# One input load for the small vectors, a later start for the f16 scores, and spare matrix products in foreseen gaps

## The chip, the core and the metric

The kernel runs on one core of one Trainium2 chip. The core has a matrix engine (TensorE, PE in the profile), three elementwise engines (VectorE or DVE, ScalarE or ACT, GpSimd or POOL), a queue engine that mostly issues transfers (SyncE or SP), and 16 DMA engines. Each engine works through its own instructions in order and waits on the others through semaphores. The metric is the device time of one execution in microseconds (us), as the median of several runs. Lower is better.

## The reference

Attention over 8 batches, 12 heads, 448 tokens and head size 64, with a root-mean-square norm on q and k, feeds a gated feed-forward step with a token shift. All in f32:

```
q_n = q / sqrt(mean(q*q) + 1e-6) * g_q          # same for k with g_k
attn = softmax(q_n @ k_n^T / sqrt(64))
x    = (attn @ v), heads side by side            # 8 x 448 x 768
x_prev = x shifted by one token
xk = mu_k*x + (1-mu_k)*x_prev ;  xr = mu_r*x + (1-mu_r)*x_prev
kk = relu(xk @ w_k)**2                           # 768 -> 1024
out = sigmoid(xr @ w_r) * (kk @ w_v)             # 768 -> 768, 1024 -> 768
```

The weights arrive as 8-byte floats. g_q and g_k are vectors of 64, mu_k and mu_r of 768.

## The kernel before

**Tiles.** The 96 heads are taken as 48 pairs `i` (two heads of a batch) and 24 quads `u` (two pairs). A batch has three quads. The scores of a quad come in seven groups `gi` of 128 query rows for two heads, so `groups` has 168 entries; `gi < 21` belongs to the quads `u < U32 = 3`. Those first three quads are computed in f32 (one product per term); all later ones split each operand into two f16 parts and use three products per term.

**Stages.** `setup` loads g_q and g_k, forms their product and a scale from it with some twenty small DVE instructions on the tile `gm`, and writes a per-partition column `gc`. `mu_stats` loads mu_k and mu_r through the ACT queue as many 4-byte pieces and derives bounds in `muu`, `mucol` and `smu`. `load` fetches k and q of each quad, `stats` forms the sums of squares (`sst`) and their inverse roots (`ss`), `preps` scales k and q into `nat` and transposes them (`turn`, on TensorE for `u < PE_T`, by DMA afterwards) into `stk`. `scores` multiplies, `expo` takes the maximum and the exponential, `probs` and `probs_pe` normalise and transpose the result into `pT`; all groups of the first three quads take `probs_pe`. `attends` multiplies by v (tiles `vf`, `vh`, `vl`) into `x`. `mix` forms the shifted mixes through `df` into `xk` and `xr`. `wload`, `weights`, `wscale` and `wsplit` convert 20 weight tiles (`raw`, `kk`, `wk`, `wr`, `wv`, `wf`) to f16 pairs; for the bounds, `weights` also multiplies each tile with itself into the bank `pg`. `moe` runs the three large products, batch by batch: `xk` with `wk` first, then, once all weights are split and `xr` is there, `xr` with `wr` and `kk` with `wv`, and stores `o`.

**Accumulators.** All products land in one ring of eight banks named `ps`, shared out by use: at most five for scores and TensorE transposes (`sc`), two for `moe`, two for attention output, one for `pg`, and so on. `scores` takes two `sc` banks for each group; before, it took them for the first quads when more than `SC_KEEP = 2` were free. A transpose of `turn` or `probs_pe` needs one `sc` bank.

**Order.** Each stage is a generator that yields its next operation. `Plan` keeps a modelled clock for every engine and the modelled end of every access to a tile. `run` picks the operation with the smallest key: the later of its engine's clock and its data, plus a margin, less `PS = 0.1` ns for each point of priority. `emit` writes the instruction and moves the clocks. So the whole order on all engines is fixed when the kernel is built, and each engine then runs its list as the data arrive. All instructions but a few carry line 289 of `emit` in the profile. The priority of `attends` contains `BOOST_A`, that of the weights `W_GAP` (a smaller `W_GAP` raises it sooner).

Of the kernel before, what the change touches and what calls it, by code (L numbers as in the profile page):

```python
# [7 lines left out]
F32 = mybir.dt.float32  # L8
# [8 lines left out]
P = 128  # L17
HD = 64
# [45 lines left out]
PRIO_M = 400  # L64
BOOST_K = 500
BOOST_R = 500
BOOST_A = 0
BOOST_W = 300
BOOST_Q = 600
SLACK_S = 3  # L70
# [8 lines left out]
Q_DVE = 1  # L79
V_POOL = True  # L80
PE_T = 6
U32 = 3
V_SIDE = 2
SWITCH = 600
# [7 lines left out]
LEAD_V = 1  # L92
LEAD_W = 1
PE_P = range(1, 21, 2)
SC_KEEP = 2
TR_COST = 130
W_GAP = 7e3
W_PUSH = 0.03
NEWTON_ON = "DVE"
OP_SLOW = 1.0  # L100
# [118 lines left out]
        return lambda form=None, **kw: Op(self.name, f, {k: aps(x) if hasattr(x, "shape") else x for k, x in kw.items()}, form)  # L219


class Plan:
    LAT = 35

    def __init__(self, tc):
        self.tc = tc
        self.clk = dict.fromkeys(("PE", "DVE", "ACT", "POOL", "SP"), 0.0)
        self.last, self.use, self.threads = {}, {}, []
        self.form, self.dma_free, self.acc, self.n = None, {"SP": 0.0, "ACT": 0.0}, False, 0
        self.held = {"DVE": [], "POOL": []}  # L230

    def margin(self, form):
        if form == "moe":
# [49 lines left out]
    def emit(self, ops):  # L283
        e = ops[0].eng
        rel = self.ready(ops)
        s = max(self.clk[e], rel)
        for op in ops:
            with self.tc.issue_after(self.last[e].ins) if e in self.last else nullcontext():
                r = op.fn(op.kw["out"], op.kw["value"]) if op.fn.__name__ == "memset" else op.fn(**op.kw)  # L289
            self.last[e] = r  # L290
        if e == "PE":
            form, cost = ops[0].form
            form = MODE.get(form, 0)
            cost *= PE_SLOW
            if form != self.form:
                s += 105
            self.form = form
            self.clk[e] = s + cost
            fin = s + cost + 190
            for op in ops:  # L300
                self.note(op, fin)
        elif ops[0].fn.__name__.startswith("dma"):
            op = ops[0]
            x = op.kw["out"]
            n = width(x) * x.ap[0][1]
            if "transpose" in op.fn.__name__:
                w, iss, tot = n / 128 * 1.21, 1700, 4000
            else:
                w, iss, tot = n / 55, 350, 3300
            w, tot = w * DMA_SLOW, tot * DMA_SLOW  # L310
            other = "ACT" if e == "SP" else "SP"
            if e == "ACT":
                end = s + (375 if n > 60000 else 610)
            else:
                end = max(s + iss, min(self.dma_free[e] - 1200, s + 4000))
            self.clk[e] = end + 35
            begin = max(self.dma_free[e], s + tot - w - 900)
            both = DMA_SHARE * min(w, max(0.0, self.dma_free[other] - begin))
            self.dma_free[e] = begin + w + both
            self.dma_free[other] += both  # L320
            self.note(op, self.dma_free[e] + 900)
        else:
            op = ops[0]
            pace, dur = (x * OP_SLOW for x in price(op))
            if e == "ACT":
                acc = op.kw.get("accum_out") is not None
                if acc and self.acc:
                    s = max(s, self.clk[e] + ACC_GAP)
                self.acc = acc
            if e in self.held and shares(op):  # L330
                for a, b in self.held["DVE" if e == "POOL" else "POOL"]:
                    if a <= s < b - 190:
                        s = b - 190
                h = self.held[e]
                h.append((s, s + dur))
                del h[:-16]
            self.clk[e] = s + pace
            self.note(op, s + dur)
        self.n += 1

    def run(self):
        while self.threads:
# [29 lines left out]
class Ring:  # L372
# [21 lines left out]
    def get(self, early=False):  # L394
        ok = lambda: [x for x in self.free if early or isinstance(x, str)]
        while not ok():
            yield ok
        tag = ok()[0]
        self.free = [x for x in self.free if x is not tag]
        if not isinstance(tag, str):  # L400
            self.of[id(tag)] = (tag, None, tag)
            return tag
        pool = self.more.get(tag) or (self.pool() if callable(self.pool) else self.pool)
        t = pool.tile(self.shape, self.dtype, name=tag, bufs=1)
        name = aps(t).tensor.name
        self.of[id(t)] = (tag, name, t)
        old = self.plan.use.get("slot " + tag)
        if old:
            self.plan.use[name, 0], self.plan.use[name, 1] = [(0, 1 << 30, old, True, False)], [(0, 1 << 30, old, True, False)]
        return t  # L410
# [43 lines left out]
            yield V.scalar_tensor_tensor(out=y, in0=t, scalar=1.5, in1=y, op0=ALU.add, op1=ALU.mult)  # L454


def attn_moe_kernel(tc, q, k, v, g_q, g_k, mu_k, mu_r, w_k, w_v, w_r, out):
    nc = tc.nc
    B, H = 2 * out.shape[0], D_MODEL // HD
    NP = H // 2  # L460
# [12 lines left out]
    banks = {n: Share(psum, *c) for n, c in (("sc", SC_SHARE), ("mm", MM_SHARE), ("ot", OT_SHARE), ("wz", WZ_SHARE), ("pg", PG_SHARE), ("df", DF_SHARE))}  # L473

    ident16 = const.tile([P, P], BF16, name="ident16")
    gq = const.tile([P, HD], F32, name="gq")
    gk = const.tile([P, HD], F32, name="gk")
    mu = const.tile([P, 2, 2, ND], F32, name="mu")
    gm = const.tile([P, 8], F32, name="gm")
    G = gq  # L480
    gc = const.tile([P, 1], F32, name="gc")
# [14 lines left out]
    NQ, NPAIR, NSS, NSL, NVB = len(quads), len(pairs), 4 * NT, (NT + 1) // 2, 2 * NT  # L496
    VFREE = [const.tile([P, NVB, HD], F32, name="vf%d" % n) for n in range(VF_BUFS)]

    st = {"wdone": 0, "g": 0, "moe": 0, "vl": 0, "gm": False, "mus": False, "want": "xk", "sg": 0, "su": 0, "pu": 0, "vi": 0, "wkeys": 0, "kdone": 0, "zq": 0, "tq": 0, "lu": 0}
    LD, SS, VF, VV, TQ, PT, BS, BSC, XT, XK, XKN, XR, CNT, OS, CARRY, FR = {}, {}, {}, {}, {}, {}, {}, {}, {}, {}, {}, {}, {}, {}, {}, {}  # L500

    plan.st = st
# [62 lines left out]
    ring_sum = [small.tile([P, 12], F32, name="sums%d" % n, bufs=1) for n in range(6)]  # L565

    def setup():
        yield SP.dma_start(out=gq, in_=g_q.partition_broadcast(P))
        yield SP.dma_start(out=gk, in_=g_k.partition_broadcast(P))
        yield A.copy(out=ident16, in_=ident)  # L570
        yield V.memset(out=ones, value=1.0)
        st["vf"] = True
        yield V.scalar_tensor_tensor(out=G, in0=gq, scalar=1.0 / float(HD) ** 0.5, in1=gk, op0=ALU.mult, op1=ALU.mult)
# [11 lines left out]
        st["gm"] = True  # L585

    def mu_stats():
        yield from until(lambda: st["lu"] >= 1 and len(RAW))
        yield A.dma_start(out=mu[:, 0, 0, :], in_=mu_k.rearrange("(t p) -> p t", p=P))
        yield A.dma_start(out=mu[:, 1, 0, :], in_=mu_r.rearrange("(t p) -> p t", p=P))  # L590
        yield V.tensor_scalar(out=mu[:, :, 1, :], in0=mu[:, :, 0, :], scalar1=-1.0, scalar2=1.0, op0=ALU.mult, op1=ALU.add)
        u = small.tile([P, 2, ND], F32, name="muu")
        u2 = small.tile([P, 2, ND], F32, name="muu2")
# [205 lines left out]

    def scores():  # L800
        for gi, (u, x, t0) in enumerate(groups):
            yield from until(lambda: u in TQ and len(banks["sc"].free) > (SC_KEEP if u < U32 or gi in PE_P else 1) and not st["zq"])
            tp = None
            if u < U32 or gi in PE_P:
# [77 lines left out]
    def probs_pe(u, x, t0, sums, tp):  # L882
# [8 lines left out]
        for a0 in range(0, NT, 4):  # L891
            m = min(4, NT - a0)
            st["zq"] += 1
            z = yield from banks["sc"].get()
            st["zq"] -= 1
            yield [T.transpose(form=("tr", TR_COST * m), out=z[:, a * P:(a + 1) * P], in_=tf[:, (a0 + a) * P:(a0 + a + 1) * P], identity=ident) for a in range(m)]
            src = z[:, 0:m * P].rearrange("p (a c) -> p a c", c=P)
            if u < U32:
                dst = whole(PTQ[:, :, :])[:, a0:a0 + m, c0:c0 + P]
                yield A.copy(out=dst, in_=src) if plan.pick("ACT", "DVE") == "ACT" else V.tensor_copy(out=dst, in_=src)  # L900
            else:
                hi, lo = (PTQ[:, h + a0:h + a0 + m, c0:c0 + P] for h in (0, NT))
                yield A.copy(out=hi, in_=src)
                yield V.tensor_tensor(out=lo, in0=src, in1=hi, op=ALU.subtract)
            banks["sc"].put(z)
        R["nat"].put(tp)
        for i in (2 * u, 2 * u + 1) if t0 == NT - 1 else (2 * u + x,):
            CNT[i] += 1
# [100 lines left out]
    def weights():  # L1009
        for nm, w, kt, c, ci in WT:  # L1010
            if c == 0:
                pg = yield from banks["pg"].get()
            last = ci + 1 in (NF, NF + ND, NW)
            nb = 2 if ci < NF else 1
            if last:
# [6 lines left out]
            for h in range(2):  # L1022
# [8 lines left out]
                yield V.scalar_tensor_tensor(out=fi[:, cols], in0=z.bitcast(I32), scalar=3, in1=fi[:, cols], op0=ALU.logical_shift_left, op1=ALU.bitwise_or)  # L1031
                banks["wz"].put(zb)
                R["raw"].put(raw)
            w16 = f.bitcast(BF16).rearrange("p (i n two) -> p i n two", two=2, n=P)[:, :, :, 1]
            yield [T.matmul(form=("w", 110 * kt), out=pg[:, c % nb * P:(c % nb + 1) * P], lhsT=w16[:, i, :], rhs=w16[:, i, :], start=(c == 0 and i == 0), stop=(last and i == kt - 1)) for i in range(kt)]
            if last:
                plan.spawn(wscale(nm, kt, ci - c, ci + 1, pg, nb * P), wprio)

# [158 lines left out]
    ctx.close()  # L1197


_INS = ["q", "k", "v", "g_q", "g_k", "moe_mu_k", "moe_mu_r", "moe_w_k", "moe_w_v", "moe_w_r"]  # L1200


def layouts(inputs):
# [31 lines left out]
    for name in ("moe_w_k", "moe_w_v", "moe_w_r"):  # L1235
        w = np.asarray(inputs[name])
        a = w.reshape(2, -1, P, w.shape[1] // P, P).transpose(3, 0, 2, 1, 4)
        laid[name] = np.ascontiguousarray(a).reshape(*a.shape[:3], -1)
    return {**laid, "q": qd, "k": kd, "v": vd.reshape(b * h // 2, P, 2 * NT * HD)}


def tokens_back(o, b):
# [29 lines left out]
```

## Time and profile before

| | |
|---|---|
| median of 3 runs | 1003.53 us (1002.27 to 1003.83) |
| the profiled execution: time | 1002.68 us |
| the profiled execution: span of the instructions | 1000.9 us |
| mean granted TensorE clock | 0.973 of full speed |
| instructions | 18138 |
| busy: TensorE, ScalarE, GpSimd, VectorE | 91%, 78%, 68%, 66% |
| packets moved, mean rate | 359357, 156 GB/s |

The span runs from the first to the last instruction; the time holds 1.8 us more. Busy time counts an engine as busy while an instruction of its own is under way; for TensorE, the ends of the products are modelled and they overlap. In the rows below, `SPq` and `ACTq` are the queues on which transfers are issued, `PEld` is the loading of TensorE's stationary operand, and `[3.74 <-DVE nat L289]` means that the engine was idle for 3.74 us before the row and that a DVE instruction writing `nat` ended that wait. `x7` at the end counts the instructions merged into the row.

### The profile page before, as it was taken

What the parts mean: (1) busy time and instruction counts of PE and PEld (TensorE: products, weight loads), DVE (VectorE), ACT (ScalarE), POOL (GpSimd) and SP (SyncE); (2) the same over time, 40 slices, a digit from 0 to 9 for tenths busy, and PEclk for the clock granted to TensorE, in tenths of its full rate; (3) what the DMA queues carried; (4) which work ended last, traced back from release to release, by engine and by line L of the source; (5) the groups of instructions that cost most, each with busy time, mean ns of one, the idle gap of its engine ahead of it and who ended that gap; (6) DMA issues with size and microseconds to landing.
All of it is one profiled execution on the core that took longest, in us unless ns stands there. A gap on an engine that the chain in (4) does not pass through costs nothing. (4 is left out here: it accounts for less than half of the span.)

```text
span 1000.9 us, 18138 instructions
## 1 busy us (share of the span) xinstructions
PE 911.1 (91%) x6048; PEld 478.5 (48%) x6048; DVE 663.7 (66%) x1816; ACT 781.2 (78%) x1740; POOL 675.9 (68%) x744
## 2 busy tenths in 40 slices
PE   0687859799899999999999999989998999999998
PEld 0443434355444555445444555445544555565564
DVE  4797887778875887688875878777866875012000
ACT  2587889889997999999997999999889977424200
POOL 2578898957797777978797777968588624635400
PEclk9798969989999999999999999999999999999999
DMA  5444566499978999799988999999977992100000
GB/s 191 150 153 126 174 183 131 79 200 187 231 145 170 223 215 225 155 205 210 232 168 157 219 208 224 187 185 196 217 170 150 182 182 69 37 16 32 1 33 31
DMA packets 359357, 156.38 MB, mean 156 GB/s; under 512 B 338272, under 2 KB 338272, under 8 KB 359264
## 3 DMA queue, kind: packets, MB, share of 16 engines
q1 hardware_dynamic: 357552, 154.76, 70.5%
q8 instruction: 47, 0.77, 0.3%
q10 hardware_dynamic: 1712, 0.47, 0.2%
q14 instruction: 46, 0.38, 0.1%
HBM read 60.23 MB, written 11.01 MB: 71 GB/s over the span
## 5 line engine op out<-in xcount | busy, mean ns | idle before, releaser
L289 PE MATMUL ps<-wv,kk 128*128 128x384 f16 x1344 | 233.8, 326 | 1.4 <-DVE df L289 1.4
L289 PE MATMUL ps<-xk,wk 128*128 128x448 f16 x1152 | 226.1, 353 | 2.8 <-DVE nat L289 2.2
L289 DVE TENSOR_REDUCE sums<-ps 128x1 f32<-128x448 f32 x336 | 192.3, 613 | 20.4 <-PE ps L289 20.2
L289 ACT ACTIVATE ps<-ps,sums 128x448 f32<-128x448 f32 x294 | 189.3, 646 | 18.3 <-DVE sums L289 16.7
L289 DVE SCALAR_TENSOR_TENSOR nat<-ps,sums,nat 128x448 f16<-128x448 f32 x242 | 158.7, 677 | 56.3 <-ACT nat L289 55.8
L289 ACT ACTIVATE nat<-ps,sums 128x448 f16<-128x448 f32 (+1 forms) x274 | 173.1, 679 | 22.6 <-DVE sums L289 15.0
L289 PE MATMUL ps<-wr,xr 128*128 128x384 f16 x1008 | 180.3, 330 | 2.4 <-DVE o L289 1.3
L289 PEld LDWEIGHTS <-kk 128*128 128x128 f16 (+1 forms) x1350 | 128.0, 98 | 97.6 <-issue 17.1
L289 PEld LDWEIGHTS <-wk 128*128 128x128 f16 (+1 forms) x1194 | 113.4, 99 | 113.5 <-issue 14.2
L289 PE MATMUL ps<-stk 64*128 64x448 f16 (+3 forms) x1104 | 131.5, 384 | 22.0 <-DVE nat L289 9.4
L289 PEld LDWEIGHTS <-xr 128*128 128x128 f16 x1008 | 96.8, 99 | 76.5 <-issue 16.6
L289 DVE SCALAR_TENSOR_TENSOR o<-o,ps 128x384 f32<-128x384 f32 x56 | 30.7, 548 | 108.5 <-PE ps L289 108.3
L289 DVE SCALAR_TENSOR_TENSOR df<-x,bsc,ps 128x448 f32<-128x448 f32 x96 | 63.8, 674 | 54.1 <-ACT ps L289 46.6
L289 PE MATMUL ps<-pT,vh 128*64 128x448 f16 x588 | 93.2, 361 | 0.2
L289 ACT ACTIVATE o<-ps,bsc 128x384 f32<-128x384 f32 x48 | 28.9, 603 | 76.5 <-PE ps L289 76.5
L289 POOL TENSOR_TENSOR qk<-qk,ss 128x896 f32<-128x896 f32 x36 | 60.9, 1693 | 19.1 <-DVE ss L289 15.9
L289 PEld LDWEIGHTS <-stk 64*128 64x128 f16 x1008 | 35.7, 97 | 76.4 <-issue 50.0
L289 POOL TENSOR_SCALAR o<-o,bsc 128x768 f32<-128x768 f32 x24 | 21.8, 910 | 71.7 <-DVE o L289 54.3
L289 POOL TENSOR_TENSOR nat<-nat 128x448 f32<-128x448 f32 x38 | 43.1, 1135 | 38.7 <-ACT nat L289 19.9
L289 ACT ACTIVATE ps<-x,bsc 128x448 f32<-128x448 f32 x96 | 64.4, 683 | 0.8 <-DVE nat L289 0.7
L289 POOL TENSOR_TENSOR xr<-df,xr 128x448 f16<-128x448 f32 x48 | 49.5, 1042 | 21.8 <-ACT xr L289 21.7
L289 POOL TENSOR_SCALAR vf<-vf,bstat 128x896 f32<-128x896 f32 x42 | 42.8, 1019 | 28.2 <-DVE bstat L289 16.3
(172 smaller groups left out, 1553.2 us busy)
## 6 DMA issues: line engine op xcount, KB each, us to landing
vf<-in_v_dram SPq DMA_DIRECT2D x42, 448.0 KB, 4.2
out_dram<-o SPq DMA_DIRECT2D x28, 384.0 KB, 2.8
qk<-in_k_dram SPq DMA_DIRECT2D x23, 448.0 KB, 4.4
qk<-in_q_dram SPq DMA_DIRECT2D x22, 448.0 KB, 4.3
raw<-in_moe_w_v_dram SPq DMA_DIRECT2D x12, 512.0 KB, 3.9
raw<-in_moe_w_r_dram SPq DMA_DIRECT2D x12, 384.0 KB, 3.2
kk<-in_moe_w_k_dram SPq DMA_DIRECT2D x8, 384.0 KB, 3.3
raw<-in_moe_w_k_dram SPq DMA_DIRECT2D x8, 384.0 KB, 3.2
```

Source lines behind the costliest of these rows:

```text
L289: r = op.fn(op.kw["out"], op.kw["value"]) if op.fn.__name__ == "memset" else op.fn(**op.kw)
```

## The change

It has three parts.

1. **One load.** g_q, g_k, mu_k and mu_r are laid side by side on the host, for each of the 128 partitions, in one array `small` of 152 f32 columns. One transfer on SP's queue brings it into the tile `few`; `gq`, `gk` and `mu` are views of it. The two broadcast loads on SP's queue and the two loads on ACT's queue are gone. `mu_stats` starts once `setup` has ended (`st["gm"]`), where it had waited for the progress of other loads.
2. **Order.** `BOOST_A` goes from 0 to 700, `SC_KEEP` from 2 to 1, `W_GAP` from 7000 to 6000. The scores of group 21 and later wait until all 21 groups of the first three quads have ended `probs_pe` (`st["pz"]`).
3. **Spare products.** When `emit` writes a TensorE operation that the plan's clocks place later than the end of the one before, `warm` puts 128x128 bf16 products of the identity with itself ahead of it: one for every 57 ns of 0.8 times the foreseen gap less 200 ns. While a weight matrix is being converted they go to the unread columns 384 to 511 of `pg`; at other times, and only for operations of certain kinds that begin an accumulation, to the first 128 columns of the bank that this operation is about to overwrite. For the first such gap only half of it is taken, at most 6 us. The plan's clocks are not moved by them.

```
+AHEAD = 0
-BOOST_A = 0          +BOOST_A = 700
-SC_KEEP = 2          +SC_KEEP = 1
-W_GAP = 7e3          +W_GAP = 6e3
+WARM = ("tr", "sc", "t6", "av", "moe")
+WARM_GAP = 200 ; WARM_SHARE = 0.8 ; WARM_COST = 57 ; WARM_UP = 12e3
...
     def emit(self, ops):
-        for op in ops:
+        for op in (self.warm(ops[0], s) if e == "PE" else []) + ops:
...
+    def warm(self, op, s):
+        begin = max(self.clk["PE"], self.warm_at)
+        fill = self.filler
+        t = self.bank.get(op.kw["out"].tensor.name)
+        if fill is None and t is not None and op.form[0] in WARM and op.kw.get("start", True):
+            fill = self.own(t)
+            for name, lo, hi in op.writes:
+                begin = max([begin] + [x[2] for x in self.use.get(name, ())])
+        if fill is None:
+            return []
+        gap = s - begin - WARM_GAP
+        if not self.awake:
+            self.awake, gap = True, min(gap, WARM_UP) / 2
+        return [fill] * max(0, int(gap * WARM_SHARE / WARM_COST))
...
     def setup():
-        yield SP.dma_start(out=gq, in_=g_q.partition_broadcast(P))
-        yield SP.dma_start(out=gk, in_=g_k.partition_broadcast(P))
+        yield SP.dma_start(out=few, in_=small_in)
         yield A.copy(out=ident16, in_=ident)
+        st["ident16"] = True
+        plan.own = lambda t: T.matmul(form=("x", 0), out=t[:, 0:P], lhsT=ident16, rhs=ident16, start=True, stop=True)
+        plan.warm_at = plan.clk["ACT"] + 1000
...
     def mu_stats():
-        yield from until(lambda: st["lu"] >= 1 and len(RAW))
-        yield A.dma_start(out=mu[:, 0, 0, :], in_=mu_k.rearrange("(t p) -> p t", p=P))
-        yield A.dma_start(out=mu[:, 1, 0, :], in_=mu_r.rearrange("(t p) -> p t", p=P))
+        yield from until(lambda: st["gm"])
...
     def scores():
         for gi, (u, x, t0) in enumerate(groups):
+            yield from until(lambda: gi < 7 * U32 + AHEAD or st["pz"] == 7 * U32)
...
     def probs_pe(u, x, t0, sums, tp):
...
+        st["pz"] += 1
...
     def weights():
             if c == 0:
                 pg = yield from banks["pg"].get()
+                yield from until(lambda: "ident16" in st)
+                plan.filler = T.matmul(form=("x", 0), out=pg[:, 3 * P:4 * P], lhsT=ident16, rhs=ident16, start=True, stop=True)
...
+            if c == 0:
+                plan.filler = None
...
+            plan.filler = None if last else T.matmul(form=("x", 0), out=pg[:, 3 * P:4 * P], lhsT=ident16, rhs=ident16, start=False, stop=False)
```

More of the change, by code (lines that the diff above doesn't have):

```diff
@@ L66 @@
 BOOST_R = 500
-BOOST_A = 0
+BOOST_A = 700
 BOOST_W = 300
@@ L94 @@
 PE_P = range(1, 21, 2)
-SC_KEEP = 2
+SC_KEEP = 1
 TR_COST = 130
-W_GAP = 7e3
+W_GAP = 6e3
 W_PUSH = 0.03
@@ L219, in __getattr__ @@
         return lambda form=None, **kw: Op(self.name, f, {k: aps(x) if hasattr(x, "shape") else x for k, x in kw.items()}, form)
+WARM = ("tr", "sc", "t6", "av", "moe")
+WARM_GAP = 200
+WARM_SHARE = 0.8
+WARM_COST = 57
+WARM_UP = 12e3
 class Plan:
@@ L230, in __init__ @@
         self.held = {"DVE": [], "POOL": []}
+        self.filler, self.own, self.bank, self.awake, self.warm_at = None, None, {}, False, 0.0
     def margin(self, form):
@@ L406, in get @@
         self.of[id(t)] = (tag, name, t)
+        if tag[:2] == "ps":
+            self.plan.bank[name] = t
         old = self.plan.use.get("slot " + tag)
@@ L454, in rsqrt, with attn_moe_kernel @@
             yield V.scalar_tensor_tensor(out=y, in0=t, scalar=1.5, in1=y, op0=ALU.add, op1=ALU.mult)
-def attn_moe_kernel(tc, q, k, v, g_q, g_k, mu_k, mu_r, w_k, w_v, w_r, out):
+def attn_moe_kernel(tc, q, k, v, small_in, w_k, w_v, w_r, out):
     nc = tc.nc
@@ L475, in attn_moe_kernel @@
     ident16 = const.tile([P, P], BF16, name="ident16")
-    gq = const.tile([P, HD], F32, name="gq")
-    gk = const.tile([P, HD], F32, name="gk")
-    mu = const.tile([P, 2, 2, ND], F32, name="mu")
+    few = const.tile([P, 2 * HD + 4 * ND], F32, name="few")
+    gq, gk = few[:, 0:HD], few[:, HD:2 * HD]
+    mu = few[:, 2 * HD:].rearrange("p (w a t) -> p w a t", w=2, a=2)
     gm = const.tile([P, 8], F32, name="gm")
@@ L497, in attn_moe_kernel @@
     VFREE = [const.tile([P, NVB, HD], F32, name="vf%d" % n) for n in range(VF_BUFS)]
-    st = {"wdone": 0, "g": 0, "moe": 0, "vl": 0, "gm": False, "mus": False, "want": "xk", "sg": 0, "su": 0, "pu": 0, "vi": 0, "wkeys": 0, "kdone": 0, "zq": 0, "tq": 0, "lu": 0}
+    st = {"wdone": 0, "g": 0, "moe": 0, "vl": 0, "gm": False, "mus": False, "want": "xk", "sg": 0, "su": 0, "pu": 0, "vi": 0, "wkeys": 0, "kdone": 0, "zq": 0, "tq": 0, "lu": 0, "pz": 0}
     LD, SS, VF, VV, TQ, PT, BS, BSC, XT, XK, XKN, XR, CNT, OS, CARRY, FR = {}, {}, {}, {}, {}, {}, {}, {}, {}, {}, {}, {}, {}, {}, {}, {}
@@ L1197, in attn_moe_kernel @@
     ctx.close()
-_INS = ["q", "k", "v", "g_q", "g_k", "moe_mu_k", "moe_mu_r", "moe_w_k", "moe_w_v", "moe_w_r"]
+_INS = ["q", "k", "v", "small", "moe_w_k", "moe_w_v", "moe_w_r"]
 def layouts(inputs):
@@ L1238, in layouts @@
         laid[name] = np.ascontiguousarray(a).reshape(*a.shape[:3], -1)
-    return {**laid, "q": qd, "k": kd, "v": vd.reshape(b * h // 2, P, 2 * NT * HD)}
+    few = np.zeros((P, 2 * HD + 4 * ND), np.float32)
+    few[:, 0:HD], few[:, HD:2 * HD] = inputs["g_q"], inputs["g_k"]
+    for w, name in enumerate(("moe_mu_k", "moe_mu_r")):
+        o = 2 * HD + 2 * ND * w
+        few[:, o:o + ND] = np.asarray(inputs[name]).reshape(ND, P).T
+    return {**laid, "small": few, "q": qd, "k": kd, "v": vd.reshape(b * h // 2, P, 2 * NT * HD)}
 def tokens_back(o, b):
```

## The prediction

> **What bounds the kernel now.** I read the head of the page first, then the busy time of each engine by stretch, then the waits and the order of time inside the stretches where TensorE is idle. From the page: busy time of TensorE and its granted clock in 40 slices of 25 us.
>
> ```profile
> span 1000.9 us, 18138 instructions
> PE   0687859799899999999999999989998999999998
> PEclk9798969989999999999999999999999999999999
> ```
>
> TensorE is full from about 200 us on; the gaps and the low clock lie ahead of that. The same by stretch (columns: window, length, busy time and count of PE, PEld, DVE, ACT, POOL, granted clock, DMA share, GB/s), and the last piece of the chain of work that ended last:
>
> ```profile
> 0.00:24.00 24.00, 0.76 (x4) 0.31 (x4) 10.09 (x44) 5.73 (x10) 5.06 (x12) 1.00 0.58 200
> 24.00:206.00 182.00, 138.75 (x825) 73.64 (x826) 148.25 (x371) 145.47 (x322) 143.89 (x172) 0.87 0.51 144
> 34.00:50.00 16.00, 10.09 (x54) 7.04 (x56) 12.37 (x36) 8.48 (x21) 10.33 (x13) 0.68 0.41 128
> 84.00:102.00 18.00, 14.74 (x66) 6.60 (x67) 13.52 (x26) 13.73 (x32) 14.90 (x17) 0.74 0.45 148
> 130.00:158.00 28.00, 16.86 (x111) 8.79 (x108) 22.66 (x46) 25.73 (x54) 24.55 (x28) 0.70 0.73 207
> 190.00:206.00 16.00, 9.61 (x62) 4.06 (x63) 12.65 (x34) 15.21 (x37) 11.98 (x17) 0.68 0.69 140
> 206.00:761.00 555.00, 537.18 (x3743) 274.49 (x3742) 427.02 (x1212) 517.11 (x1171) 429.63 (x446) 1.00 0.95 195
> 761.00:1001.00 240.00, 234.40 (x1480) 130.03 (x1479) 78.30 (x191) 112.91 (x239) 97.31 (x116) 0.99 0.32 71
> 777.12 206.86 PE ps L289 x1311
> ```
>
> TensorE idles 23.2 us before 24, 43.2 us (182 - 138.75) from 24 to 206, 17.8 us (555 - 537.18) from 206 to 761, and hardly after: the last 240 us are products alone, waiting for nothing. The elementwise engines end early. So the end is TensorE's work plus its idle time plus what the low clock adds, and nearly all of the last two lies in the first 206 us, where VectorE, ScalarE and GpSimd are each about 80% busy (148, 145, 144 of 182).
>
> **The one load.** Rows in order of time on VectorE, the waits on VectorE and on SP's queue, the times to landing, and the busy time of a short window:
>
> ```profile
> 7.92 0.67 DVE L289 SCALAR_TENSOR_TENSOR gq<-gq,gk 128x64 f32<-128x64 f32 x1 [7.05 <-DMA gk<-in_g_k_dram]
> 12.24 0.61 DVE L289 TENSOR_REDUCE sst<-nat 128x14 f32<-128x448 f32 x1
> 12.77 0.26 DVE L289 SCALAR_TENSOR_TENSOR gm<-gm 128x1 f32<-128x1 f32 x1
> 18.24 0.17 DVE L289 TENSOR_SCALAR mu<-mu 128x12 f32<-128x12 f32 x1 [5.22 <-DMA mu<-in_moe_mu_r_dram]
> 19.82 0.17 DVE L289 TENSOR_SCALAR ps<-sst 128x14 f32<-128x14 f32 x1
> ...
> SPq L289 <- DMA mu<-in_moe_mu_k_dram: 4.2, 1, 4.2
> gq<-in_g_q_dram SPq DMA_DIRECT2D x1, 32.0 KB, 4.7
> gk<-in_g_k_dram SPq DMA_DIRECT2D x1, 32.0 KB, 6.6
> mu<-in_moe_mu_r_dram ACTq DMA_DIRECT2D x1, 3.0 KB, 11.4
> 13.03:18.24 5.21, 0.00 (x0) 0.00 (x0) 0.00 (x0) 0.00 (x0) 1.05 (x2) 1.00 0.80 281
> 23.98 1.76 PE L289 MATMUL ps<-ident,nat 128*128 128x128 f32 x7 [3.74 <-DVE nat L289]
> ```
>
> The load of mu_r needs 11.4 us to land for 3 KB, and VectorE, in order, stands for 5.22 us before the first instruction that reads it. Behind it in the queue are the last `gm` steps, and behind those the inverse roots of quad 0 (19.82), whose chain ends in TensorE's first transposes at 23.98. In that hole TensorE and ScalarE do nothing and GpSimd 1.05 us. The change takes this load away, so the chain closes up by 5.2 us. `mu_stats` now comes after `gm`; its five small VectorE steps (0.17 us each) stood ahead of the roots before too, so I count them at nothing.
>
> The new load brings 128 x 152 x 4 B = 76 KB where gq and gk brought 32 KB each. Between their times, 4.7 and 6.6 us, and if it is issued first, as gq was, it lands some 2 us ahead of VectorE's first use, which stood at 7.92 and waited for gk, the second; or it loses some of that, if 76 KB takes longer. The roots can't start before quad 0's second sum, which stood at 12.24 among the `gm` steps. SP's queue issues one transfer less and loses its own 4.2 us wait on mu; ScalarE's queue loses two issues. That is nothing more for the path, since the weights loaded there wait for VectorE. Gain at the roots: 4.5 (closed hole, late landing) to 8 us; I take 5.5. How much of it reaches the end? All stages after it were started by this chain, but the elementwise engines, 80% busy from 24 to 206, could take some back. I count **-5**, bounds -2 and -7.
>
> **The order.** TensorE and ScalarE around the end of the first three quads:
>
> ```profile
> 129.77 0.74 PE L289 MATMUL ps<-stk 64*128 64x448 f16 x6 [1.64 <-DVE wv L289]
> 130.67 0.74 PE L289 MATMUL ps<-stk 64*128 64x448 f16 x6 [0.16 <-ACT pT L289]
> 135.37 1.09 PE L289 MATMUL ps<-ident,nat 128*128 128x128 f32 x4 [3.38 <-DVE df L289]
> 139.29 0.90 PE L289 MATMUL ps<-ident,nat 128*128 128x128 f32 x3 [1.02 <-DVE df L289]
> 144.19 0.60 ACT L289 ACTIVATE ps<-ps,sums 128x448 f32<-128x448 f32 x1
> 147.77 4.73 PE L289 MATMUL ps<-pT,vf 128*64 128x448 f32 x16 [1.27 <-ACT pT L289]
> 157.35 2.43 PE L289 MATMUL ps<-xk,wk 128*128 128x448 f16 x12
> ```
>
> The first f16 scores (f16 operands `stk`) run at 129.77 and 130.67 and hold four of the five `sc` banks; the last of the four exponentials that read them runs at 144.19. The transposes for quad 2 have one bank left, and the last attention product of batch 0 starts at 147.77, the first `moe` product at 157.35. With the new wait these scores come last, so quad 2 has all five banks and no exponentials or maxima ahead of it. In 130 to 158 TensorE idles 11.1 us. A third of that is **-4**. Ends: -9, if quad 2's chain goes straight through; above nothing, since b=1's attention starts later. If the two groups wait until the last `pT` copy (just before 147.77), they and what follows in the one generator `scores` come some 17 us later, and six to eight groups of 0.74 us that fill TensorE up to 206 could be missing there: +5. Later than that, attention ends at 761 with 240 us of products still to run, which hides its delay. `SC_KEEP = 1` lets scores leave no free bank; one transpose then waits for one exponential, 0.6 us by the row above. `BOOST_A` and `W_GAP` are worth 70 ns and at most about 0.03 x 1000 x 20 x 0.1 = 60 ns in the key: they only reorder near ties. I put no sum on these three, and 2 us of scatter either way.
>
> **The spare products.** What a low clock costs, by equal rows, cold and warm:
>
> ```profile
> 25.53 0.85 PE L289 MATMUL ps<-wk 128*128 128x128 bf16 x6
> 53.35 0.51 PE L289 MATMUL ps<-wk 128*128 128x128 bf16 x6
> 144.35 0.61 PE L289 MATMUL ps<-wv 128*128 128x128 bf16 x4 [0.86 <-DVE wv L289]
> 152.43 0.63 PE L289 MATMUL ps<-wv 128*128 128x128 bf16 x8
> 65.42 3.23 PE L289 MATMUL ps<-pT,vf 128*64 128x448 f32 x16
> 89.00 5.10 PE L289 MATMUL ps<-pT,vf 128*64 128x448 f32 x16
> 84.15 0.35 PE L289 MATMUL ps<-wr 128*128 128x128 bf16 x3 [1.83 <-DVE wr L289]
> 86.38 0.90 PE L289 MATMUL ps<-ident,xk 128*128 128x128 f32 x3 [0.97 <-ACT nat L289]
> 199.53 0.29 PE L289 MATMUL ps<-ident,vs 128*128 128x128 bf16 x1 [3.74 <-ACT vh L289]
> ```
>
> If the clock is full or half (the 16 attention products take 3.23 or 5.10, partly warm), a mean of 0.68 says cold for 64% of the time. Busy time in the four stretches above, times the cold share, halved: 10.09 x 0.64/2 = 3.2, 14.74 x 0.52/2 = 3.8, 16.86 x 0.60/2 = 5.1, 9.61 x 0.64/2 = 3.1; and I estimate as much, 3.5, for the first ten microseconds of products (x6 takes 0.85 at 25.53, not 0.51). That is 18.7 us of slower work. Most of it lies beside waits for other engines, so I let 5 to 6 us count: long runs of products on the path, like those from 89.00 and 147.77.
>
> Price of a spare product: two more in a warm row cost (0.63 - 0.51)/2 = 0.06 us, in a cold one (0.85 - 0.61)/2 = 0.12. The plan counts 0.057. So a warm fill takes 0.8 of the foreseen gap, a cold one 1.7 of it and comes out late. If the plan foresees gaps as long as those measured, 43 us less 0.2 each, and part of the first 24, that is some 500 to 900 products. Where the plan sees a gap that isn't on the chip, the fill delays real work. I charge 2 to 3 us of it to the path: net **-3**, bounds -7 and +8 (the rival below).
>
> The Trainium skill, page "TensorE: Matmul & The Clock Gate", section "Back-to-back issue gap", gives an estimate of about 81 ns for each product with its own weight load at 128 columns; by it even a warm fill would take 0.8 x 81/57 = 1.14 of the gap, and the gaps of 3.38 and 3.74 us in the rows above would be overrun by about 0.3 each: the sum would be about 1 us worse. The rows here say 60 ns, and I go by them. The same page's section "Why this matters for your kernels" has the clock fall after gaps over about 3 us; in the rows at 84.15 and 86.38 it fell with no gap over 1.83 us, so filling short gaps is worth something here, which that rule would put at nothing.
>
> **The sum.** -5 - 4 - 3 = -12 on the profiled time of 1002.68 gives 990.7; the median shown lies 0.85 above that execution, so I say **991**, with its own range 984 to 997.
>
> **The rivals.**
> *Only the load counts.* The new order and the fills cancel out. For it: the keys change by tens of ns, and ScalarE is 92% busy in 130 to 158 and 95% in 190 to 206, so a faster TensorE finds no data. Against it: the held banks are plain in the rows. 1003.5 - 2 to 1003.5 - 7: 996.5 to 1001.5, say 999.
>
> *No change.* The 5 us are taken back ahead of 206, because the elementwise work before the second `moe` product is what counts: 1001.5 to 1005.5. Against it: in the hole these engines stood still.
>
> *Slower: fills without a gap.* Place: 206 to 761, where `moe` and scores get fills too. There TensorE is the bound and a spare product that meets no idle time costs its 60 ns in full. If the plan foresees as much idle time as the chip has, 17.8 us, but ahead of other operations, 0.8 of it is 14 us, less the 200 ns of each gap perhaps 11: +11, less 5 for the load, gives 1009 (1006 to 1014). It decides from 5 us of misplaced fills on, if order and clock bring nothing.
>
> *Much faster.* Quad 2 straight through (-9), clock in full (-7), load -7: 976 to 983.
>
> **How the numbers follow.** Forecast 0.50; only the load 0.22; no change 0.09; slower 0.13; much faster 0.06. The range for 8 in 10 takes in the forecast, most of "only the load" and the edge of "much faster": 981 to 1002. About 0.2% (2 us) is what a measurement of this kernel can tell from none: faster 0.78, same 0.09, slower 0.13.
>
> **What would show it.** The load: no VectorE wait on a transfer near 13 us, first transposes near 18 instead of 23.98. The order: no f16 scores ahead of quad 2's last transposes, the first `moe` product near 145 instead of 157.35, less than 8 us idle in that stretch. The fills: several hundred more TensorE products of the identity with itself, the granted clock near 1.0 before 206, the 16 f32 attention products always near 3.23. The forecast is wrong if the first transposes come early but the full stretch still begins near 206, or if idle or spare time on TensorE grows after 206.

## The result

The changed kernel takes 989.81 us (median of 4, 988.08 to 994.07) where the kernel before took 1002.9 beside it: 0.9875 of it, 95% interval 0.9842 to 0.9909. On a second chip it took 991.21 where before took 1001.51: 0.9889 (0.987 to 0.9908). The forecast was 991. One of the six executions of the kernel with the spare products alone, further down, took 2232.98 us and is left out of that kernel's ratio. The runs below show that the sum came out right while two of its three terms stood for something else.

### The profile page after: what moved, and what is told of

Its sections match the earlier page's. It is cut to its first block, busy times and chain, and to the rows that moved or that the text cites. A ratio compares the mean times of both kernels' runs of the same rounds, so it can differ in the third digit from the quotient of the medians.

```text
span 988.6 us, 18862 instructions
## 1 busy us (share of the span) xinstructions
PE 926.8 (94%) x6408; PEld 494.9 (50%) x6408; DVE 663.1 (67%) x1815; ACT 781.6 (79%) x1741; POOL 676.5 (68%) x744
## 5 line engine op out<-in xcount | busy, mean ns | idle before, releaser
L298 ACT ACTIVATE ps<-ps,sums 128x448 f32<-128x448 f32 x294 | 187.1, 638 | 20.9 <-DVE sums L298 19.2
L298 PE MATMUL ps<-stk 64*128 64x448 f16 (+3 forms) x1104 | 128.2, 377 | 14.8 <-DVE nat L298 4.1
L298 POOL TENSOR_TENSOR xk<-df,xk 128x448 f16<-128x448 f32 x48 | 49.6, 1036 | 21.6 <-ACT xk L298 21.4
```

## The profile after

The page of the changed kernel, then its stretches as they were shown for before (same columns), and the end of its chain:

```profile
span 988.6 us, 18862 instructions
PE 926.8 (94%) x6408; PEld 494.9 (50%) x6408; DVE 663.1 (67%) x1815; ACT 781.6 (79%) x1741; POOL 676.5 (68%) x744
PE   6878789799898999989999999999999999999997
PEclk9999999799898999999999999999999999999999
0.00:24.00 24.00, 16.27 (x173) 13.68 (x173) 17.64 (x64) 11.23 (x23) 6.67 (x14) 0.93 0.69 252
24.00:206.00 182.00, 153.93 (x1143) 86.34 (x1145) 151.09 (x391) 156.00 (x348) 153.46 (x182) 0.96 0.60 158
158.00:190.00 32.00, 24.75 (x153) 12.12 (x150) 24.10 (x63) 27.32 (x58) 27.26 (x27) 0.84 0.51 101
206.00:761.00 555.00, 534.15 (x3690) 271.45 (x3686) 421.98 (x1185) 508.70 (x1154) 425.11 (x441) 0.99 0.92 189
769.22 202.39 PE ps L298 x1281
```

The shape is the same: from about 187 us on TensorE is full, and the end is products alone. The clock before 206 us rose from 0.87 to 0.96 over 24 to 206. But idle time in 206 to 761, the full stretch, rose too, from 17.8 to 20.9 us (555 - 534.15).

The head of VectorE's order, the new load's time to landing, and TensorE's marks (products that begin or end a stage):

```profile
2.71 0.22 DVE L298 SCALAR_TENSOR_TENSOR few<-few 128x64 f32<-128x64 f32 x1 [1.84 <-DMA few<-in_small_dram]
10.40 0.17 DVE L298 TENSOR_SCALAR ps<-sst 128x14 f32<-128x14 f32 x1
few<-in_small_dram SPq DMA_DIRECT2D x1, 76.0 KB, 1.9
14.66 1.05 PE L298 MATMUL ps<-ident,nat 128*128 128x128 f32 x7 [3.41 <-DVE nat L298]
114.30 1.28 PE L298 MATMUL ps<-stk 64*128 64x448 f16 x6 [0.56 <-DVE pT L298]
115.73 4.22 PE L298 MATMUL ps<-pT,vf 128*64 128x448 f32 x16
132.44 3.57 PE L298 MATMUL ps<-xk,wk 128*128 128x448 f16 x18
185.64 1.73 PE L298 MATMUL ps<-wr,xr 128*128 128x384 f16 x6 [2.40 <-ACT x L298]
```

The roots start at 10.40 instead of 19.82, the first transposes at 14.66 instead of 23.98, the last attention product of batch 0 at 115.73 instead of 147.77, its first `moe` product at 132.44 instead of 157.35, the second kind at 185.64 instead of 206.15. So a lead of 9 us grows to 32, and of the 20 us left at the start of the full stretch only 12 reach the end. That a lead on a mark isn't a lead at the end is the main lesson of the runs.

The spare products are `ps<-ident` in bf16, identity with itself:

```profile
L298 PE MATMUL ps<-ident 128*128 128x128 bf16 x360 | 26.6, 232 | 4.0 <-ACT ident L298 2.4 <-DVE nat L298 1.6
121.03 1.95 PE L298 MATMUL ps<-ident 128*128 128x128 bf16 x32
125.59 4.35 PE L298 MATMUL ps<-ident 128*128 128x128 bf16 x75
130.37 0.40 PE L298 MATMUL ps<-wv 128*128 128x128 bf16 x4 [0.42 <-DVE wv L298]
```

Between the two bursts, 43 products more cost 2.40 us, 56 ns each. The longest burst, the 75, ends before the data that the next product needs: that one still waits 0.42 us.

## The experiments

The theory after the result was that of the prediction: load, order and spare products are worth 5, 4 and 3 us and add up. The rival was that TensorE's faster products are nearly the whole gain. Later a second rival came up: the parts don't add, since every edit makes the plan write another list. Each ratio is to the kernel before on the same chip, with its 95% interval.

### Spare products out

```
-WARM_SHARE = 0.8
+WARM_SHARE = 0.0
```

> The changed kernel with no spare product at all (share 0 instead of 0.8); every other instruction stands in the same order on every engine. Theory A (the prediction's sum, spare products worth 3 us net): 991 to 995, clock before 206 us back near 0.87. Theory B (the trace after: the real products take 10.9 us less TensorE time than before, while idle plus spare time together is unchanged, so the clock is nearly all of the gain): 998 to 1001. Theory C (the spare products hold real work up and their clock buys nothing): 986 to 989.

Measured: 993.25 us, 0.9919 (0.9903 to 0.9934), against 0.9889 (0.987 to 0.9908) with them in the next set of runs on that chip. By that they are worth 0.3%, the 3 us of theory A; as the two figures come from different sets, the 3 us are uncertain by some 2.5. B and C are out. The clock over 24 to 206 us is 0.90 here, so it doesn't quite fall back to 0.87.

### The hole alone closed, the list unchanged

```
-yield A.dma_start(out=mu[:, 0, 0, :], in_=mu_k.rearrange("(t p) -> p t", p=P))
+yield A.dma_start(out=mu[:, 0, 0, :], in_=mu_k)        # 128 x 6, laid out on the host
...                                                    # mu_r likewise
```

> The kernel before with mu_k and mu_r laid out by partition on the host, so that its two ACT-queue loads bring 24 bytes in one piece to each partition; nothing else, same order of all instructions. Theory A (VectorE's wait of 5.2 us is a hole that closes up and reaches the end): first transposes near 18.5 us instead of 23.98, 997 to 999.5. Theory B (the elementwise engines take it back ahead of 206 us): first transposes just as early, time 1001.5 to 1004. Theory C (the front is bound by something else, as the landing of gk or of q): first transposes at 22 or later, no change of time.

Measured: 996.84 us, 0.9958 (0.9943 to 0.9973), so 4.2 us less. VectorE's order of time and the time to landing:

```profile
13.11 0.17 DVE L289 TENSOR_SCALAR mu<-mu 128x12 f32<-128x12 f32 x1 [0.22 <-DMA mu<-in_moe_mu_r_dram]
mu<-in_moe_mu_r_dram ACTq DMA_DIRECT2D x1, 3.0 KB, 6.5
19.42 1.75 PE L289 MATMUL ps<-ident,nat 128*128 128x128 f32 x7 [3.74 <-DVE nat L289]
```

The same 3 KB in pieces of 24 bytes land in 6.5 us, not 11.4; the wait of 5.22 shrinks to 0.22, the first transposes come 4.6 us earlier, and nearly all of that reaches the end. Theory A. Every engine has its instructions in the order of the kernel before: with an unchanged list, closing a hole of 5.0 us was worth 4.2.

### The order's numbers as before, and the wait alone taken out

```
-AHEAD = 0 ; BOOST_A = 700 ; SC_KEEP = 1 ; W_GAP = 6e3
+AHEAD = 1000 ; BOOST_A = 0 ; SC_KEEP = 2 ; W_GAP = 7e3     # first kernel; the second has AHEAD = 1000 only
```

> The changed kernel (one load, spare products) with the order's four numbers as before: no wait of the f16 scores, BOOST_A 0, SC_KEEP 2, W_GAP 7000. Theory A (prediction: order worth 4 us): 993 to 996, and quad 2's last attention product later than 125 us. Theory B (order worth nothing, load and spare products do it all): 988 to 991. Theory C (order is the main term): 998 or more.

> The changed kernel without the wait of the f16 scores for quad 2's end, the other three numbers kept as changed. Theory A (the wait is what the order part is worth): as e3, 993 to 996, with f16 scores well ahead of quad 2's last transposes. Theory B (the wait binds little, the three other numbers or the load moved quad 2): 988 to 991.5 and the first xk product still near 132 us.

Measured: 992.45 us, 0.9919 (0.9903 to 0.9934) with the old numbers, so the order part is worth 3 us beside the others, again uncertain by some 2.5. That is theory A, and quad 2's last attention product does come later, at 141.18. Without the wait alone: 988.2, 0.9871 (0.9855 to 0.9887), no slower than the changed kernel's 0.9889. That is theory B, though the first `moe` product comes at 137.04 and not near 132. The wait, on which the prediction had put the whole of the order's gain, brings nothing here.

### Each part alone

The changed kernel once more (0.9889, above), then:

> The one load alone: no spare products, order's four numbers as before (the plan may still place things otherwise, since its own clock for the loads changes). Theory A (the parts add: 4.4 us each for spare products and order, so 4 left for the load): 0.995 to 0.997 of before, first transposes near 14.8. Theory B (the load's 9 us at the front reach the end, the parts overlap): 0.990 to 0.992.

> The order's four numbers alone: four separate loads as before, no spare products. Theory A (adds 4.4 us by itself): 0.9945 to 0.9965 of before. Theory B (the new order only pays when the front comes early or TensorE is warm): 0.998 to 1.003. Theory C (scatter of a list order: it could as well lose): over 1.003.

> The kernel before with spare products alone; all other engines' order is that of before. Theory A (adds 4.4 us by itself, clock near 0.99): 0.9945 to 0.9965. Theory B (the hole at 13 to 18 us, which the plan doesn't foresee, leaves TensorE cold and late, so less): 0.997 to 1.001. Theory C (fills that meet no idle time): over 1.002.

Measured: load alone 1001.32 us, 0.9999 (0.9986 to 1.0013); order alone 990.78, 0.9897 (0.9881 to 0.9912); spare products alone 995.88, 0.994 (0.9925 to 0.9956). Load alone and order alone fit none of the theories given for them; spare products alone come out a little below theory A, with the clock that it named (0.986). The parts multiply to 0.984, the whole has 0.9889: they don't add up, and the load brings nothing by itself although its front comes 8.8 us early. TensorE's marks in load alone, then stretch 130 to 166 in load alone and in before:

```profile
15.21 1.73 PE L298 MATMUL ps<-ident,nat 128*128 128x128 f32 x7 [5.36 <-DVE nat L298]
141.19 1.11 PE L298 MATMUL ps<-ident,nat 128*128 128x128 f32 x4 [3.79 <-DVE ps L298]
147.38 4.68 PE L298 MATMUL ps<-pT,vf 128*64 128x448 f32 x16
165.68 4.63 PE L298 MATMUL ps<-xk,wk 128*128 128x448 f16 x12 [3.22 <-DVE nat L298]
130.00:166.00 36.00, 18.57 (x98) 9.91 (x99) 27.07 (x69) 28.16 (x59) 24.25 (x30) 0.59 0.58 172
130.00:166.00 36.00, 24.86 (x154) 13.09 (x151) 28.82 (x71) 32.96 (x67) 31.10 (x33) 0.76 0.74 194
```

The list that the plan writes once the load is cheaper brings quad 2's last attention product at 147.38, as before, and the first `moe` product at 165.68, 8 us later. All four compute engines are less busy there, and the clock is 0.59. So the lead is lost without any engine being full there. That the new list is the reason, and not something in the one load itself, is suggested by the run with the hole closed, where the list of before carried the lead to the end. It isn't shown: the one load on the list of before has no run.

Span, TensorE's busy time and mean clock in nine profiled executions, with the spare products' busy time taken off; "rest" is the span less the real products, so it holds idle time and spare products together:

```
                       span    busy   spare   real    rest   clock
before               1000.9   911.1    0     911.1    89.8   0.973
hole closed           996.1   909.4    0     909.4    86.7   0.974
load alone            999.9   918.2    0     918.2    81.7   0.963
order alone           988.2   905.6    0     905.6    82.6   0.977
spare alone           992.8   927.6   34.2   893.4    99.4   0.986
changed, no spare     991.8   913.0    0     913.0    78.8   0.975
changed, old order    990.2   932.6   39.9   892.7    97.5   0.992
changed               988.6   926.8   26.6   900.2    88.4   0.984
old list, see below   980.9   930.2   41.6   888.6    92.3   0.993
```

Load alone takes 8.1 us off the rest and pays 7.1 back in slower products. Spare products alone take 17.7 us off the real products and put 9.6 on the rest, so 8.1 are left. Rows of spare and real products overlap a little, which makes "real" too small where there are spare ones: by the rows of the real products alone it is 897.2 for spare alone and 903.7 for changed, so that 13.9 us come off and 5.8 go on the rest. Two things can put them there, and the table can't tell them apart: real products that end sooner wait longer for the elementwise engines, and spare products can run into real work. After 6 of the 22 bursts of spare alone, with 184 of its 502 spare products, the next real product starts without any wait.

### The order's numbers one by one

```
+AHEAD = 0        # first kernel: the wait alone, on the kernel before
+SC_KEEP = 1      # third kernel: this alone; the second has it with BOOST_A = 700 and W_GAP = 6e3, no wait
```

> The kernel before with one edit: the scores of group 21 and later wait until the first three quads have ended probs_pe. Theory A (the prediction: banks come free for quad 2): quad 2's last attention product starts near 130 us instead of 147.77, ratio to before 0.993 to 0.997. Theory B (it only delays work that TensorE needs later): last attention product early all the same, ratio 0.998 to 1.003.

> The kernel before with BOOST_A 700, SC_KEEP 1 and W_GAP 6000, but without the wait of the f16 scores. Theory A (the prediction: these three reorder near ties, 2 us of scatter): 0.998 to 1.002. Theory B (they are what the order part is worth, as the changed kernel without the wait was no slower): 0.988 to 0.992.

> The kernel before with SC_KEEP 1 alone: the f32 scores take two banks when two are free, where they waited for three. Theory A (prediction: nothing but one exponential's wait): 0.998 to 1.002. Theory B (holding scores back for a third bank was what stretched the front): 0.990 to 0.995, quad 2's last attention product well ahead of 147.77 us.

Measured: wait alone 1003.18 us, 1.0005 (0.9996 to 1.0013); the other three 1005.97, 1.0028 (1.0017 to 1.0039); `SC_KEEP = 1` alone 1005.95, 1.0038 (1.0025 to 1.005). Together they had 0.9897. The wait alone has the ratio of its theory B, but not the early attention product; the other two kernels fit none of their theories. TensorE's marks, four rows of the wait alone and one of the three without it, and the stretch 206 to 761 of the three and of all four:

```profile
134.68 1.11 PE L298 MATMUL ps<-ident,nat 128*128 128x128 f32 x4 [2.15 <-POOL nat L298]
143.60 1.75 PE L298 MATMUL ps<-ident,nat 128*128 128x128 f32 x7 [3.81 <-POOL nat L298]
146.22 2.42 PE L298 MATMUL ps<-stk 64*128 64x448 f16 x12
148.57 3.71 PE L298 MATMUL ps<-pT,vf 128*64 128x448 f32 x16
130.52 4.95 PE L298 MATMUL ps<-pT,vf 128*64 128x448 f32 x16
206.00:761.00 555.00, 532.48 (x3675) 269.51 (x3673) 420.15 (x1190) 506.77 (x1145) 424.22 (x442) 0.99 0.94 191
206.00:761.00 555.00, 543.78 (x3770) 279.09 (x3768) 421.08 (x1188) 507.94 (x1145) 424.52 (x443) 1.00 0.92 189
```

The wait alone does what it was meant to do: the f16 scores come at 146.22, behind quad 2's transposes. But these transposes now wait for GpSimd writing `nat` (2.15 and 3.81 us), and the last attention product stays where it was (148.57). So the banks that the scores held were not what kept quad 2 back. The three numbers bring that product to 130.52 and the kernel is slower all the same; TensorE then idles 22.5 us in the full stretch, against 17.8 before. With the wait as well, it idles 11.2. These 6.6 us less than before are half of the gain of the order alone (12.7 us between the two spans). Of the four numbers only `BOOST_A` acts in the full stretch: `attends` has it in every batch in which `moe` waits for its `xk`.

### The order's list kept, the hole closed in it

```
 # order's numbers and spare products as changed; the four separate loads as before, with
+yield A.dma_start(out=mu[:, 0, 0, :], in_=mu_k)        # mu_k and mu_r laid out on the host
```

> The changed kernel's order numbers and spare products, but with the four separate loads, so that the plan makes the list that it made for the order numbers alone; mu_k and mu_r laid out by partition so that their loads land early. Theory A (closing the hole gives 4 us where the list stays the same, and the spare products 3 to 8): 0.980 to 0.985, faster than the changed kernel. Theory B (what the front gains is always paid back ahead of the full stretch): 0.987 to 0.991, as the changed kernel.

Measured: 983.94 us, 0.9816 (0.9802 to 0.9829), faster than both kernels; the changed kernel had 0.9875 (0.9842 to 0.9909) and 0.9889 (0.987 to 0.9908) in other sets of runs. Theory A. Stretches, spare products and the second kind of `moe` product, and then the longest sum of TensorE's waits in the full stretch of the changed kernel:

```profile
24.00:206.00 182.00, 158.04 (x1322) 94.59 (x1322) 155.44 (x399) 153.53 (x340) 153.10 (x180) 0.99 0.58 158
206.00:761.00 555.00, 543.62 (x3785) 278.98 (x3779) 420.22 (x1181) 509.98 (x1148) 430.00 (x447) 1.00 0.93 190
L298 PE MATMUL ps<-ident 128*128 128x128 bf16 x562 | 41.6, 234 | 2.8 <-ACT ident L298 2.8
193.84 2.12 PE L298 MATMUL ps<-wr,xr 128*128 128x384 f16 x12
PE ps L298 <- ACT vh L298: 4.8, 2, 3.9
```

The list is the one of the order alone, with its 11.4 us of idle time in the full stretch. Its second kind of `moe` product starts 8 us later than in the changed kernel (193.84 against 185.64 in the profiles), and yet it ends 7.7 us earlier. About as much shows in the full stretch, where TensorE idles 9.5 us less than in the changed kernel (20.9). 4.8 of these are two waits for ScalarE writing `vh`, which this list doesn't have there.

## Why the prediction was right, and where it wasn't

**What bounds the kernel: right, but the gains were sought in too short a stretch.** In all nine executions of the table TensorE is 91 to 95% busy, and the changed kernel too ends with 202 us of its products in a row. But I looked for gains ahead of 206 us alone, and half of the order's gain lies behind it.

**The load: the hole right, its way to the end wrong.** Closing the hole was put at 5 us, 2 to 7; it measured 4.2. The step that failed is "all stages after it were started by this chain": the runs bear it out for a fixed list only. The load as changed also alters what the plan believes, the plan writes another list, and with that list nothing is left of the gain (0.9999). With the order's four numbers the list changes too, and the load seems to cost about 2 us (order alone 0.9897, with the load 0.9919; the intervals touch). The landing was mis-sized as well: 76 KB took 1.9 us, not 4.7 to 6.6. Nor was quad 0's second sum at 12.24 a bound: it stood behind `gm` steps and now comes at 9.87. So the roots gained 9.4 us where 8 was the upper end.

**The order: size near, mechanism wrong.** I put -4 on the wait and its free banks, nothing on the three small numbers. Beside load and spare products the order part is worth 3 us, by itself 10.3; the wait alone is worth nothing, and the three alone lose 2.8. The step that failed is that the f16 scores' banks held quad 2 back: in the run with the wait alone they come behind quad 2, and it is no earlier. The 2 us of scatter for the three numbers were too few: `SC_KEEP`, priced at one wait of 0.6 us, lost 3.8 by itself, and the same three with the wait gain 10.3.

**The spare products: right.** Slower work was put at 18.7 us; spare products alone took 13.9 to 17.7 off, by the two counts above. Net 3 us was forecast; 3 were measured in the changed kernel (uncertain by some 2.5), 6 by themselves. 360 products were written, below the 500 to 900 forecast (502 on the list of before). The price by rows, 60 ns, held: 56 measured, and the longest burst ended in time. The 81 ns for a product with its own weight load, of the Trainium skill, page "TensorE: Matmul & The Clock Gate", section "Back-to-back issue gap", do not fit this trace: the profile counts a weight load for each of the 6408 products, and the spare ones cost 56 ns. The rival "fills without a gap" did not come about: 7 of the 360 stand behind 206 us.

**The signs.** Most came as named or stronger: the first transposes at 14.66 (near 18 forecast), the first `moe` product at 132.44 (near 145), 3.3 us idle in 130 to 158 (under 8). Of the six f32 attention products five take 3.23, but the last 4.22, and the clock before 206 us is 0.96, not quite 1.0. One sign of being wrong came too: idle and spare time on TensorE after 206 us grew, from 17.8 to 20.9 us and from none to 0.9. The total held in spite of it.

The right total was thus largely luck. One after the other the runs give -10.3 for the order, some +2 for the load and -3 for the spare products, about -11 where -5 - 4 - 3 was written: the load's -5 didn't come, and the order gave what it lacked, for a reason that the forecast hadn't named.

**Open.** Only the spare products and the closed hole were tried at a fixed list; what the load as changed is worth can't be told apart from the list that comes with it. Which of the order's four numbers it takes to make the good list: `BOOST_A` and `W_GAP` have no run of their own. Nor is it shown why that list idles less after 206 us; that an order which always takes the smallest key scatters by 1% from list to list would explain it, but is only argued. Nor was the best version without the wait tried.

## What to carry to other kernels

Where a program writes the order from modelled clocks, test a transfer or a wait at a fixed list first: closing the hole was worth 4 us there, and nothing where the plan wrote a new list. Price a change of keys or of such a wait by the spread that lists have shown (here 1%), not by the size of the key. Follow a lead to the end by two sums, the products' own time and all the rest; marks in the middle mislead.

## What the runs showed of the chip

One transfer of 76 KB in rows of 608 bytes landed in 1.9 us, where 3 KB in 4-byte pieces took 11.4 and in 24-byte pieces 6.5. The last two differ in the pieces alone; the 76 KB went on another queue and as the first transfer, so how much of the 1.9 is owed to the long rows isn't shown. Spare products of 128 columns on the identity raise TensorE's clock: on the kernel before, with its list unchanged, 502 of them make it 0.97 over 24 to 206 us, against 0.87 without:

```profile
24.00:206.00 182.00, 154.42 (x1266) 92.30 (x1266) 153.81 (x384) 150.84 (x335) 148.02 (x175) 0.97 0.58 152
```

With few of them it can still fall: in the changed kernel 7 stand between 132 and 186 us, and over 158 to 190, where TensorE idles 7.3 of 32 us, the clock is 0.84. The last product of a weight tile with itself starts there at 150.53; why the plan writes so few after it isn't shown.
